# Attention, rational MLP and PReLU MLP in one kernel: shared, larger rooms for turned score halves, and mirrored and producing key chunks taken in turns

## The chip, the cores and the metric

The kernel runs on one core of one Trainium2 chip. Its time is the device time of one execution in microseconds (us). Before the change three runs gave 1598.0, 1600.2 and 1601.96 us, with a median of 1600.2 us. The rows below come from one more execution, which was profiled and took 1600.62 us.

## The reference

Three stages follow one another. Attention without softmax, in two batches of 3008 rows, model width 256, key width 64:

```python
scores = scale * np.matmul(z, z.transpose(0, 2, 1))   # scale = 1 / 3008
attn = np.maximum(scores, 0.0) ** 2
out = np.matmul(attn, v)
x = u * out
```

Then, on the 6016 rows of both batches, an MLP of hidden width 2048 with a rational activation, and a second one with a PReLU:

```python
h = x @ w_in                                          # MLP 1
P = a[0] + a[1] * h + a[2] * h2 + a[3] * h3           # h2, h3: powers of h
Q = 1.0 + np.abs(b[0]) * np.abs(h) + np.abs(b[1]) * h2
x = (P / (Q + 1e-06)) @ w_out
h = x @ w_in2                                         # MLP 2
y = (np.maximum(h, 0.0) + alpha * np.minimum(h, 0.0)) @ w_out2
```

Queries and keys are the same z, so the score matrix of a batch is symmetric: the block of queries j against keys i is the transpose of the block of queries i against keys j.

## The kernel before, in words

**Arithmetic.** Each float32 operand is split into a high and a low part (`hi`, `lo`), and a product is made of three matmuls: high by high, high by low, low by high. Splitting a tile is one cast (ACT, L118) and one subtraction (DVE, L121).

**Attention.** A batch has NQ = 6 rows (query blocks j = 0 to 5 of 512 queries, the last of 448) and NKP = 12 key chunks kp of 256 keys; chunks 2i and 2i+1 make key block i. For each chunk TensorE (PE) makes the scores (L393, L394, four matmuls into two PSUM tiles `s`), ACT applies relu (L397) and square (L400) into a tile `r` of the tag "t", ACT and DVE split it into `ahi` and `alo`, and three chunks later (LAG_A) PE adds the chunk's product with the values `vt` to the row's accumulator `acca` (12 matmuls, L437 and L446). At the end of a row DVE multiplies by u (`ut`, L482).

**Mirrored chunks, second batch alone** (`FOLD`, `folded`). A row j of the second batch makes no scores for key blocks i < j. It takes them from row i, which had made the same block the other way round: row i is then *producing*. A producing chunk (`turn_block`, L323) sends `r` through two DMA transposes as 16-bit halves into a tile `xt` (L333), and `save_turned` (L337) writes `xt` with two DMAs to a DRAM tile `rt` (L341). A mirrored chunk (`load_turned`, L346) brings the halves back into a tile `xd` with two DMAs (L351), and `a_turned` (L357) puts them together in a tile `rr` of tag "t" by a copy on ACT (L362) and one on DVE (L363). Row j has 2j mirrored chunks, 2 that lie on the diagonal, and 10 - 2j producing ones. All these DMAs are issued by SyncE (SP), in order; a wait at one of them holds all that stand behind it on SP.

**The rooms.** `xt` and `xd` have two buffers each (XT, XD). Tag "t" has six (TT), for `r` and `rr`, three tiles of each MLP step (`sq`, `ab`, `t`), and `dec`, in which a block of weights is decoded. An `r` that is producing is held until its transposes have landed; a `dec` that is spilled to DRAM (`wd`) until that DMA has landed.

**Order.** `a_stream` yields after each chunk. Beside it, `weights_due` and `spill_w` decode weights from step to step, and from step HEAD = 36 of 145 on, 40 steps of MLP 1 are spread evenly over the attention steps: PE h (L417 to L419, 12 matmuls) and PE acc (L437, L446, 12 matmuls), seven DVE operations of 128x1024. Their weights come as `w<-wd` loads from the POOL queue (L774). After the attention the rest of MLP 1 and all of MLP 2 run alone. The program is written in this order; a scheduler then orders each engine's instructions and gives each tile its buffer.

Around the change `fetch` (L675) issues the load of the next mirrored chunk, at most AHEAD = 1 beyond the one in use, and `drain` takes the rows' ends at chunks NKP-2 and NKP-1.

Of the kernel before, what the change touches and what calls it, by code (L numbers as in the profile page):

```python
# [11 lines left out]
U16 = mybir.dt.uint16  # L12
# [3 lines left out]
DRAM = bass.MemoryType.DRAM  # L16


BIG, HL, TT, RAW, ZP, XP = 24, 7, 6, 2, 8, 4

XT, XD, AHEAD = 2, 2, 1

FOLD = ((1, 0),)

# [4 lines left out]
LAG_A, LAG_M = 3, 2  # L29
# [23 lines left out]
def relu2_attention_rational_mlp_prelu_mlp(  # L53
# [15 lines left out]
    nc = tc.nc  # L69
    P = 128  # L70
# [6 lines left out]
    QB = 512  # L77
    NQ = -(-S // QB)
    NK = -(-S // P)
    NKP = NK // 2  # L80
# [15 lines left out]
    zctx = ExitStack()  # L96
    zp = zctx.enter_context(tc.tile_pool(name="zp", bufs=ZP))
    wr = zctx.enter_context(tc.tile_pool(name="wr", bufs=WR))
    xdp = zctx.enter_context(tc.tile_pool(name="xdp", bufs=XD))
    late = {}  # L100

    def raw_tile(nm, early=False):

        if early:
            return big.tile([P, 1024], F32, tag="big", name=nm)
        return tmp.tile([P, 1024], F32, tag="raw", name=nm, bufs=RAW)
# [34 lines left out]
    def load_v(b, kp):  # L141

        if b == 0:
            raw = raw_tile("vraw", True)
        else:
            raw = wr.tile([P, 1024], F32, tag="wr", name="vraw")
        r3 = raw.rearrange("p (c d) -> p c d", c=4)
        r0 = kp * 2 * P
        load_rows(r3, v[b], r0, min(S - r0, 4 * P))
        vraw[b, kp] = r3  # L150
# [97 lines left out]
    def load_z(b, g):  # L248

        raw = raw_tile("zraw", b == 0)  # L250
        n = qn[g]
        nc.sync.dma_start(out=raw[:, 0:n], in_=zt[b, :, g * QB : g * QB + n])
        if n % P:
            nc.sync.dma_start(out=raw[:, n : n + HALF], in_=zt[b, :, S - HALF : S])
            n += HALF
        t = zp.tile([P, QB], F32R, tag="z", name="zA")
        with tc.high_priority(EARLY):
            nc.vector.tensor_copy(t[:, 0:n], raw[:, 0:n])
            nc.vector.tensor_tensor(
                t[HALF:P, 0:n], raw[HALF:P, 0:n], t[HALF:P, 0:n].bitcast(F32), ALU.subtract  # L260
            )
        if (b, g) == (0, 0):
            zB[b, g] = zp.tile([P, QB], F32R, tag="z", name="zB")
            nc.scalar.copy(zB[b, g][HALF:P, 0:n], raw[HALF:P, 0:n])
            nc.vector.tensor_tensor(
                zB[b, g][0:HALF, 0:n], raw[0:HALF, 0:n], t[0:HALF, 0:n].bitcast(F32), ALU.subtract
            )
        zA[b, g] = t


    blocks = [(b, j) for b in range(B) for j in range(NQ)]
# [4 lines left out]
    xd = {}  # L276
# [39 lines left out]
    def folded(b, i, j):  # L316
        return i < j and any(b == fb and i >= f0 for fb, f0 in FOLD)

    turned = {}
    halves = {}  # L320
    unsaved = []

    def turn_block(b, j, kp, r):  # L323

        kb, k0 = kp // 2, kp % 2 * 2 * P
        if (b, j, kb) not in turned:
            turned[b, j, kb] = dr.tile([2, QB, QB], U16, name=f"rt{b}_{j}_{kb}")
        x = xdp.tile([P, 8, 2 * P], U16, tag="xt", name="xt", bufs=XT)
        ru = r.bitcast(U16)
        w = 0  # L330
        for i in range(2):
            rows = min(P, S - (2 * kp + i) * P)
            nc.sync.dma_start_transpose(out=x[:, :, w : w + rows], in_=ru[0:rows, i, :])  # L333
            w += rows
        unsaved.append((turned[b, j, kb], k0, w, x))
# [10 lines left out]
    def load_turned(b, j, kp):  # L346
        n = qn[j]
        q0 = kp % 2 * 2 * P
        d = xdp.tile([P, 2, 2, QB], U16, tag="xd", name="xd", bufs=XD)
        for h in range(2):  # L350
            nc.sync.dma_start(  # L351
                out=d[:, h, :, :n],
                in_=turned[b, kp // 2, j][h, q0 : q0 + 2 * P, :n].rearrange("(c p) k -> p c k", p=P),
            )
        halves[b, j, kp] = d
# [13 lines left out]
    def a_scores(b, j, kp):  # L369
# [43 lines left out]
        if folded(b, j, kp // 2):  # L413
            turn_block(b, j, kp, r)
# [16 lines left out]
    def pairs(acc, w, hi, lo, n, first, last, both=2):  # L431

        hi, lo = ([x[i] if type(x) is list else x[:, i, :n] for i in range(2)] for x in (hi, lo))
        for i in range(2):
            for e in range(2):
                for k in range(2):
                    nc.tensor.matmul(  # L437
                        acc[:, e, :n],
                        w[:, k, i, e * P : (e + 1) * P],
                        hi[i],  # L440
                        start=first and i == 0 and k == 0,
                        stop=False,
                    )
        for i in range(both):
            for e in range(2):
                nc.tensor.matmul(  # L446
                    acc[:, e, :n],
                    w[:, 0, i, e * P : (e + 1) * P],
                    lo[i],
                    start=False,  # L450
                    stop=last and i == both - 1,
                )

    def a_values(b, j, kp):
        n = qn[j]
        if kp == 0:

            two = j == 1 and not opened
            acc_a[b, j] = psa.tile([P, ND, QB], F32, tag=f"acc{two:d}", name="acca")
        acc = acc_a[b, j]  # L460
        hi, lo = ahl.pop((b, j, kp))
        vk = vt[b, kp]
        last = kp == NKP - 1
        pairs(acc, vk, hi, lo, n, kp == 0, last, 1 if last else 2)

    def a_u(b, j):
        n = qn[j]
        t = tmp.tile([P, ND, QB], F32, tag="raw", name="ut", bufs=RAW)
        if b == 0 and j < RAW:

            nc.gpsimd.tensor_copy(t[:, 0, 0:1], zA[0, NQ - 1][:, 0:1].bitcast(F32))
        nc.sync.dma_start(
            out=t[:, :, :n],
            in_=ut_in[b, :, j * QB : j * QB + n].rearrange("(e p) s -> p e s", p=P),
        )
        uts[b, j] = t

    def a_end(b, j):
        n = qn[j]
        t = uts.pop((b, j))  # L480
        with tc.high_priority(EARLY):
            nc.vector.tensor_tensor(t[:, :, :n], acc_a[b, j][:, :, :n], t[:, :, :n], ALU.mult)  # L482
        xd[b, j] = dr.tile([P, ND, QB], F32, name=f"xd{b}_{j}")
        nc.sync.dma_start(out=xd[b, j][:, :, :n], in_=t[:, :, :n])
# [185 lines left out]
    def a_stream():  # L670

        pend = []
        coming = [(b, j, kp) for b, j in blocks for kp in range(2 * j) if folded(b, kp // 2, j)]

        def fetch(b, j, kp):  # L675
            while coming and len(halves) < AHEAD + folded(b, kp // 2, j) and (
                coming[0][:2] == (b, j) or coming[0][:2] == (b, j + 1) and kp >= NKP - 2
            ):
                load_turned(*coming.pop(0))

        def drain(upto):
            while len(pend) > upto:
                q, kp = pend.pop(0)
                a_values(*q, kp)
                if kp == NKP - 2:
                    a_u(*q)
                if kp == NKP - 1:
                    a_end(*q)

        for q in blocks:  # L690
            b, j = q
            if q == (0, 0):
                load_z(0, 0)
                load_z(0, 1)
                load_v(0, 0)
                split_v(0, 0)
            a_begin(b, j)
            for kp in range(NKP):
                if q == (0, 0) and kp % 2 == 0:
                    for g in {0: (2,), 2: (3, 4), 4: (5,)}.get(kp, ()):  # L700
                        load_z(0, g)
                    if kp + 2 < NKP:
                        load_v(0, kp + 2)
                        split_v(0, kp + 2)
                fetch(b, j, kp)
                a_scores(b, j, kp)
                save_turned(int(folded(b, j, kp // 2)))
                pend.append((q, kp))
                drain(LAG_A)
                if j == NQ - 1 and b + 1 < B:  # L710
                    if kp % 2 == 1:
                        load_z(b + 1, kp // 2)

                k0 = kp - LAG_A - 1 if j == NQ - 1 else kp + NKP - LAG_A - 1
                b1 = b + (j == NQ - 1)
                if (j == NQ - 1 or j == 0) and 0 < b1 < B and k0 % 2 == 0:
                    if 0 <= k0 < NKP:
                        split_v(b1, k0)
                    if 0 <= k0 + 2 < NKP:
                        load_v(b1, k0 + 2)  # L720
                yield
        drain(0)
        yield

# [145 lines left out]
```

## Time and profile before

| | |
|---|---|
| median of three runs | 1600.2 us |
| the profiled execution | 1600.62 us, its span 1598.7 us |
| PE busy | 1539.4 us (96% of the span) |
| DVE busy | 1413.9 us (88%) |
| ACT busy | 1172.8 us (73%) |
| POOL busy | 90.5 us (6%) |
| DMA, queue of SP | 93.67 MB, 21.8% of 16 engines' span |
| DMA, queue of POOL | 62.94 MB, 13.4% |

An engine's busy time is the time in which it executes; PE's instructions are pipelined, so that a PE that is always busy does one matmul of 128x512 in about 0.22 us although each lasts 0.39. PEclk is the TensorE clock that was granted, as a share of full speed (2.4 GHz; 0.50 is 1.2 GHz). The DMA share is the busy time of the core's 16 DMA engines over the stretch, and can pass 1 where packets of two queues overlap on an engine. A wait is put down to what ended it. The six rows of the second batch end where DVE multiplies by u: at 421.2, 490.9, 575.1, 641.0, 710.0 and 781.1 us; the first of them begins at 340.1 us.

### The profile page before, as it was taken

What the parts mean: (1) busy time and instruction counts of PE and PEld (TensorE: products, weight loads), DVE (VectorE), ACT (ScalarE), POOL (GpSimd) and SP (SyncE); (2) the same over time, 40 slices, a digit from 0 to 9 for tenths busy, and PEclk for the clock granted to TensorE, in tenths of its full rate; (3) what the DMA queues carried; (4) which work ended last, traced back from release to release, by engine and by line L of the source; (5) the groups of instructions that cost most, each with busy time, mean ns of one, the idle gap of its engine ahead of it and who ended that gap; (6) DMA issues with size and microseconds to landing.
All of it is one profiled execution on the core that took longest, in us unless ns stands there. A gap on an engine that the chain in (4) does not pass through costs nothing.

```text
span 1598.7 us, 18271 instructions
## 1 busy us (share of the span) xinstructions
PE 1539.4 (96%) x6776; PEld 1271.4 (80%) x6776; DVE 1413.9 (88%) x1524; ACT 1172.8 (73%) x1405; POOL 90.5 (6%) x159
## 2 busy tenths in 40 slices
PE   9999999998989889888999999999999999999999
PEld 7887888786768667667788888888888888888888
DVE  8989989896979788999999998999989899998864
ACT  8989988897877878777676676667667676666644
POOL 1021000000001001101200000000000000000000
PEclk9999999998999899999999999999999999999999
DMA  6364132569897878676700010100001000001000
GB/s 203 101 208 148 59 106 73 163 148 228 235 210 209 175 221 157 192 197 214 259 2 27 27 40 1 40 12 28 27 27 40 1 27 28 35 1 40 14 1 23
DMA packets 155784, 157.76 MB, mean 99 GB/s; under 512 B 74016, under 2 KB 124720, under 8 KB 155696
## 3 DMA queue, kind: packets, MB, share of 16 engines
q1 hardware_dynamic: 134928, 93.67, 21.8%
q0 software_dynamic: 20768, 62.94, 13.4%
q8 instruction: 53, 0.87, 0.2%
q14 instruction: 35, 0.29, 0.1%
HBM read 92.94 MB, written 45.74 MB: 87 GB/s over the span
## 4 chain that ended last, share of the span: by engine, by line
PE 67%; DVE 11%; issue 9%; DMA 5%; ACT 5%; POOL 1%; SPq 0%; POOLq 0%; DVEq 0%; ACTq 0%
PE acc L437 18%; PE h L417 9%; PE h L419 9%; PE h L418 9%; PE acc L446 9%; PE acca L437 6%; PE acca L446 3%; DVE alo L121 2%; DMA wd<-dec 1%; PE s L393 1%; PE s L394 1%; DMA xt<-r 1%; PE acce L427 1%; DVE t L577 1%; ACT ahi L118 1%
## 5 line engine op out<-in xcount | busy, mean ns | idle before, releaser
L437 PE MATMUL acc<-ghi,w 128*128 128x512 f32 (+1 forms) x1472 | 365.9, 387 | 1.7 <-DVE ghi L575 1.7
L437 PEld LDWEIGHTS acc<-ghi,w 128*128 128x128 f32 x1472 | 275.3, 188 | 57.3 <-DVE ghi L575 1.6
L437 PE MATMUL acca<-ahi,vt 128*128 128x512 f32 (+1 forms) x1152 | 294.8, 394 | 10.5 <-ACT ahi L118 6.9
L417 PE MATMUL h<-xhi,w 128*128 128x512 f32 (+1 forms) x768 | 295.8, 386 | 4.1 <-DVE t L568 2.1
L418 PE MATMUL h<-xlo,w 128*128 128x512 f32 (+1 forms) x768 | 295.7, 385 | 1.1 <-DVE xlo L121 1.1
L419 PE MATMUL h<-xhi,w 128*128 128x512 f32 (+1 forms) x768 | 295.7, 385 | 0.0
L437 PEld LDWEIGHTS acca<-ahi,vt 128*128 128x128 f32 x1152 | 220.2, 192 | 58.4 <-ACT ahi L118 10.5
L446 PE MATMUL acc<-glo,w 128*128 128x512 f32 (+1 forms) x736 | 199.9, 390 | 10.5 <-DVE glo L578 10.3
L621 ACT ACTIVATE m<-h,sal 128x512 f32<-128x512 f32 (+1 forms) x192 | 127.4, 681 | 111.3 <-PE h L419 109.9
L561 ACT ACTIVATE sq<-h 128x1024 f32<-128x1024 f32 (+1 forms) x96 | 97.1, 1011 | 149.7 <-PE h L419 141.0
L417 PEld LDWEIGHTS h<-xhi,w 128*128 128x128 f32 x768 | 144.1, 188 | 35.4 <-issue 4.1
L446 PEld LDWEIGHTS acc<-glo,w 128*128 128x128 f32 x736 | 137.5, 188 | 41.9 <-DVE glo L578 14.9
L418 PEld LDWEIGHTS h<-xlo,w 128*128 128x128 f32 x768 | 144.1, 188 | 29.4 <-DVE xlo L121 1.9
L419 PEld LDWEIGHTS h<-xhi,w 128*128 128x128 f32 x768 | 144.1, 188 | 27.6
L121 DVE TENSOR_TENSOR glo<-m,ghi 128x1024 fp32r<-128x1024 f32 (+1 forms) x96 | 115.2, 1200 | 55.2 <-PE acc L437 42.0
L622 DVE SCALAR_TENSOR_TENSOR m<-h,sg,m 128x512 f32<-128x512 f32 (+1 forms) x192 | 138.1, 735 | 16.8 <-ACT m L621 15.3
L446 PE MATMUL acca<-alo,vt 128*128 128x512 f32 (+1 forms) x552 | 149.9, 389 | 0.0
L121 DVE TENSOR_TENSOR alo<-r,ahi 128x1024 fp32r<-128x1024 f32 (+2 forms) x103 | 122.9, 1195 | 17.9 <-PE acc L437 8.0
L397 ACT ACTIVATE r<-s 128x512 f32<-128x512 f32 (+1 forms) x184 | 104.2, 595 | 42.5 <-DMA xt<-r 24.3
L575 DVE SCALAR_TENSOR_TENSOR ghi<-t,sc,sq 128x1024 fp32r<-128x1024 f32 (+1 forms) x96 | 120.8, 1258 | 13.1 <-ACT sq L571 7.1
L565 DVE SCALAR_TENSOR_TENSOR ab<-sq,cb,ab 128x1024 f32<-128x1024 f32 (+1 forms) x96 | 120.8, 1258 | 9.9 <-ACT ab L562 9.7
L577 DVE SCALAR_TENSOR_TENSOR t<-t,sc,ab 128x1024 f32<-128x1024 f32 (+1 forms) x96 | 120.9, 1260 | 1.8
(96 smaller groups left out, 2222.8 us busy)
## 6 DMA issues: line engine op xcount, KB each, us to landing
w<-wd POOLq DMA_DIRECT2D x64, 512.0 KB, 4.9
rt<-xt SPq DMA_DIRECT2D x50, 256.0 KB, 3.1
wd<-dec POOLq DMA_DIRECT2D x48, 256.0 KB, 4.2
xd<-rt SPq DMA_DIRECT2D x40, 256.0 KB, 3.6
wraw<-in_moe_w_in_dram POOLq DMA_DIRECT2D x16, 512.0 KB, 4.3
wraw<-in_moe_w_out_dram POOLq DMA_DIRECT2D x16, 512.0 KB, 4.5
x2d<-x SPq DMA_DIRECT2D x11, 512.0 KB, 2.9
xr<-x2d SPq DMA_DIRECT2D x11, 512.0 KB, 3.3
```

The source lines that it names most:

```text
L121: nc.vector.tensor_tensor(dst_lo, src, dst_hi.bitcast(F32), ALU.subtract)
L397: nc.scalar.activation(r[:, i, :n], s, AF.Relu, scale=1.0 / S)
L417: nc.tensor.matmul(acc, w_hi, hi, start=first, stop=False)
L418: nc.tensor.matmul(acc, w_hi, lo, start=False, stop=False)
L419: nc.tensor.matmul(acc, w_lo, hi, start=False, stop=last)
L437: nc.tensor.matmul(acc[:, e, :n], w[:, k, i, e * P : (e + 1) * P], hi[i], start=first and i == 0 and k == 0, stop=False,)
L446: nc.tensor.matmul(acc[:, e, :n], w[:, 0, i, e * P : (e + 1) * P], lo[i], start=False, stop=last and i == both - 1,)
L565: nc.vector.scalar_tensor_tensor(ab, sq, b1, ab, ALU.mult, ALU.add)
L575: nc.vector.scalar_tensor_tensor(hi, t, a0, sq, ALU.add, ALU.mult)
L577: nc.vector.scalar_tensor_tensor(t, t, a0, ab, ALU.add, ALU.subtract)
L621: nc.scalar.activation(t[:, i], h, AF.Copy, scale=sal[:, f : f + 1])
L622: nc.vector.scalar_tensor_tensor(t[:, i], h, sg[:, f : f + 1], t[:, i], ALU.mult, ALU.max)
```

## The change

Three edits. (1) `xt` and `xd` share one tag "xx" of six buffers, and tag "t" gets seven buffers rather than six. All three kinds of tile take 4 KB of each partition, so this needs 12 KB more. (2) The ring in which POOL's queue keeps its DMA descriptors shrinks from the default of 16384 bytes of each partition to 4096, which frees those 12 KB. (3) A row of the second batch takes its mirrored chunks and the others (diagonal and producing) in turns, in proportion, and not the mirrored ones first. Where the position in the row matters and not the chunk (first and last matmul of the accumulator, u, the row's end, `fetch`, the loads of the first batch's last row), the code now goes by the position. The first batch's order stays.

With the new rule the rows of the second batch are, mirrored chunks marked with an apostrophe: row 0: 0 to 11; row 1: 2 0' 3 4 5 6 7 1' 8 9 10 11; row 2: 4 0' 5 6 1' 7 8 2' 9 10 3' 11; row 3: 6 0' 7 1' 8 2' 9 3' 10 4' 11 5'; row 5: 10 0' 1' 2' 3' 4' 11 5' 6' 7' 8' 9'. Before, all ran from 0 to 11.

```diff
-BIG, HL, TT, RAW, ZP, XP = 24, 7, 6, 2, 8, 4
-XT, XD, AHEAD = 2, 2, 1
+BIG, HL, TT, RAW, ZP, XP = 24, 7, 7, 2, 8, 4
+XX, AHEAD = 6, 1
+RING = 4096
...
-    xdp = zctx.enter_context(tc.tile_pool(name="xdp", bufs=XD))
+    xdp = zctx.enter_context(tc.tile_pool(name="xdp", bufs=XX))
...
+    def in_turns(b, j):
+        first = [kp for kp in range(NKP) if folded(b, kp // 2, j)]
+        rest = [kp for kp in range(NKP) if kp not in first]
+        order, nf = [], len(first)
+        while first or rest:
+            ahead = len(first) * (NKP - nf) > len(rest) * nf
+            order.append((first if ahead else rest).pop(0))
+        return order
+
+    order = {q: in_turns(*q) for q in blocks}
...
-        x = xdp.tile([P, 8, 2 * P], U16, tag="xt", name="xt", bufs=XT)
+        x = xdp.tile([P, 8, 2 * P], U16, tag="xx", name="xt")
...
-        d = xdp.tile([P, 2, 2, QB], U16, tag="xd", name="xd", bufs=XD)
+        d = xdp.tile([P, 2, 2, QB], U16, tag="xx", name="xd")
...
-        last = kp == NKP - 1
-        pairs(acc, vk, hi, lo, n, kp == 0, last, 1 if last else 2)
+        first, last = kp == order[b, j][0], kp == order[b, j][-1]
+        pairs(acc, vk, hi, lo, n, first, last, 1 if kp == NKP - 1 else 2)
...
-        coming = [(b, j, kp) for b, j in blocks for kp in range(2 * j) if folded(b, kp // 2, j)]
-        def fetch(b, j, kp):
+        coming = [(*q, kp) for q in blocks for kp in order[q] if folded(q[0], kp // 2, q[1])]
+        def fetch(b, j, kp, pos):
             while coming and len(halves) < AHEAD + folded(b, kp // 2, j) and (
-                coming[0][:2] == (b, j) or coming[0][:2] == (b, j + 1) and kp >= NKP - 2
+                coming[0][:2] == (b, j) or coming[0][:2] == (b, j + 1) and pos >= NKP - 2
             ):
...
-            for kp in range(NKP):
+            for pos, kp in enumerate(order[q]):
...
-    nc = _bacc.Bacc("TRN2", target_bir_lowering=False, num_devices=1)
+    nc = _bacc.Bacc("TRN2", target_bir_lowering=False, num_devices=1, dynamic_dma_scratch_size=RING)
```

How the instructions stand now, at three places. First SP in row 0 of the second batch, before, around key block 3 (in a name such as `rt1_0_3` stand the batch, the row and the key block; the numbers after `xt` and `r` tell the chunks apart):

```order
L333 DMA_TRANSPOSE xt_3259<-r_3245 128x8x128 x2
L333 DMA_TRANSPOSE xt_3291<-r_3276 128x8x128 x2
L341 DMA rt1_0_2_3185<-xt_3259 64x8x256 x2
L341 DMA rt1_0_3_3290<-xt_3291 64x8x256 x2
L333 DMA_TRANSPOSE xt_3322<-r_3308 128x8x128 x2
L351 DMA xd_3583<-rt1_0_1_3069 128x2x512
L341 DMA rt1_0_3_3290<-xt_3322 64x8x256
L333 DMA_TRANSPOSE xt_3396<-r_3381 128x8x128 x2
```

And the same place of the change:

```order
L346 DMA_TRANSPOSE xt_3259<-r_3245 128x8x128 x2
L346 DMA_TRANSPOSE xt_3291<-r_3276 128x8x128 x2
L354 DMA rt1_0_2_3185<-xt_3259 64x8x256 x2
L346 DMA_TRANSPOSE xt_3322<-r_3308 128x8x128 x2
L354 DMA rt1_0_3_3290<-xt_3291 64x8x256 x2
L354 DMA rt1_0_3_3290<-xt_3322 64x8x256 x2
L346 DMA_TRANSPOSE xt_3396<-r_3381 128x8x128 x2
L346 DMA_TRANSPOSE xt_3444<-r_3430 128x8x128 x2
```

The transposes of `r_3308` stood behind the two saves of `xt_3291`, which wait for that tile's own transposes; now they stand ahead of them.

Second, SP in row 2 of the second batch, before, from the row's loads to its third producing chunk:

```order
L351 DMA xd<-rt_0_3_3290 128x2x512 x4
L333 DMA_TRANSPOSE xt<-r 128x8x128 x4
L341 DMA rt_2_3_4475<-xt 64x8x256 x4
L333 DMA_TRANSPOSE xt<-r 128x8x128 x2
L341 DMA rt_2_4_4536<-xt 64x8x256
```

And of the change, the same producing chunks:

```order
L346 DMA_TRANSPOSE xt<-r 128x8x128 x2
L364 DMA xd<-rt_1_2_3737 128x2x512 x2
L354 DMA rt_2_3_4352<-xt 64x8x256 x2
L346 DMA_TRANSPOSE xt<-r 128x8x128 x2
L354 DMA rt_2_3_4352<-xt 64x8x256 x2
L346 DMA_TRANSPOSE xt<-r 128x8x128 x2
L364 DMA xd<-rt_1_2_3737 128x2x512 x2
```

Loads of mirrored chunks (`xd`) stood ahead of the row's transposes and behind them; now they stand between the pairs.

Third, PE at the start of row 2 of the second batch, before (`vt_2613`, `vt_2616` and `vt_2721` are the values of key chunks 0, 1 and 2, `vt_2790` and `vt_2793` those of 4 and 5):

```order
L437 MATMUL acca_4337<-ahi_4219,vt_2613 128x512 x8
L437 MATMUL acc1_3773<-ghi_4177,w_3885 128x512 x2
L446 MATMUL acca_4337<-alo_4220,vt_2613 128x512 x4
L437 MATMUL acca_4337<-ahi_4247,vt_2616 128x512 x8
L446 MATMUL acca_4337<-alo_4248,vt_2616 128x512 x4
L437 MATMUL acc1_3773<-ghi_4177,w_3885 128x512
L437 MATMUL acca_4337<-ahi_4271,vt_2721 128x512 x8
```

And of the change:

```order
L450 MATMUL acca_4356<-ahi_4223,vt_2790 128x512 x8
L459 MATMUL acca_4356<-alo_4224,vt_2790 128x512 x4
L450 MATMUL acca_4356<-ahi_4251,vt_2613 128x512 x8
L459 MATMUL acca_4356<-alo_4252,vt_2613 128x512 x4
L406 MATMUL s_4411<-zA_2649,zA_2761 128x512
L407 MATMUL s_4411<-zB_4210,zA_2761 128x512
L406 MATMUL s_4415<-zA_2649,zA_2761 128x512
L407 MATMUL s_4415<-zB_4210,zA_2761 128x512
L450 MATMUL acca_4356<-ahi_4279,vt_2793 128x512 x8
```

The row began with the products of mirrored chunks one after another; now products of a diagonal and a mirrored chunk, and new scores, follow one another.

## Rows read from the trace of the kernel before

**Rows 1.** Windows: second batch's rows 0 to 5, the rest; PEclk, DMA share, GB/s last

```profile
340.10:421.20 81.10, 73.46 (x311) 59.62 (x311) 64.24 (x65) 64.39 (x79) 6.51 (x11) 0.94 1.00 223
421.20:490.90 69.70, 63.42 (x269) 50.96 (x269) 58.61 (x62) 56.32 (x69) 4.71 (x8) 0.95 0.90 209
490.90:575.10 84.20, 74.60 (x309) 59.17 (x307) 70.26 (x78) 61.78 (x72) 9.46 (x15) 0.94 0.83 205
575.10:641.00 65.90, 61.33 (x262) 48.48 (x262) 60.57 (x65) 53.77 (x62) 5.92 (x11) 1.00 0.75 175
641.00:710.00 69.00, 60.39 (x248) 46.68 (x248) 64.07 (x76) 52.42 (x61) 6.59 (x11) 0.98 0.64 183
710.00:781.10 71.10, 64.00 (x283) 54.44 (x282) 63.56 (x65) 52.82 (x58) 10.48 (x19) 0.95 0.68 215
781.10:1598.00 816.90, 810.57 (x3654) 679.36 (x3652) 722.42 (x721) 528.39 (x622) 4.77 (x9) 1.00 0.09 29
```

**Rows 2.** Timeline of PE: start, length, the instruction, idle before it and what ended it

```profile
389.45 0.80 PE L393 MATMUL s<-zA 128*128 128x512 f32 x1 [7.38 <-ACT r L397]
...
747.37 0.80 PE L446 MATMUL acc<-glo,w 128*128 128x512 f32 x1 [4.84 <-DVE glo L578]
```

**Rows 3.** Windows around those four stalls, columns as in Rows 1

```profile
380.00:396.00 16.00, 8.62 (x29) 6.59 (x27) 10.69 (x12) 6.42 (x11) 0.00 (x0) 0.68 0.92 216
465.00:478.00 13.00, 7.44 (x25) 5.64 (x24) 7.85 (x7) 6.85 (x9) 0.00 (x0) 0.74 1.16 250
540.00:555.00 15.00, 8.36 (x25) 6.35 (x24) 7.28 (x9) 7.46 (x10) 0.07 (x1) 0.66 0.90 161
740.00:755.00 15.00, 10.16 (x37) 8.63 (x36) 11.34 (x12) 10.48 (x11) 1.07 (x2) 0.77 0.71 227
```

**Rows 4.** Waits from 340.1 to 781.1: total us, times, longest

```profile
ACT r L397 <- DMA xt<-r: 24.3, 5, 8.7
```

**Rows 5.** Timeline of ACT and of SP around 380 us

```profile
379.04 1.08 ACT L400 ACTIVATE r<-r 128x1024 f32<-128x1024 f32 x1
388.80 1.09 ACT L397 ACTIVATE r<-s 128x512 f32<-128x512 f32 x2 [8.69 <-DMA xt<-r]
...
375.70 7.41 SPq L341 DMA_DIRECT2D rt<-xt  x4
383.82 2.67 SPq L333 DMA_TRANSPOSE xt<-r  x2
```

**Rows 6.** SP's own waits, 340 to 790: total us, times, longest

```profile
SPq L351 <- DVE rr L363: 75.2, 22, 7.7
SPq L341 <- DMA xt<-r: 44.8, 23, 7.5
```

**Rows 7.** Timeline of SP, 450 to 475 and 525 to 553

```profile
460.40 10.86 SPq L333 DMA_TRANSPOSE xt<-r  x4
...
537.82 2.76 SPq L333 DMA_TRANSPOSE xt<-r  x2
548.15 0.59 SPq L341 DMA_DIRECT2D rt<-xt  x1
```

**Rows 8.** Line L333: the transposes, from issue to landing

```profile
DMA to landing us min/median/max: 3.1/4.5/9.4
```

**Rows 9.** DVE's timeline at the fourth stall, and tile xd from 736 to 750

```profile
745.54 0.67 DVE L363 COPY rr<-xd 128x896 uint16<-128x896 uint16 x1 [3.38 <-DMA xd<-rt]
...
DMA to landing us min/median/max: 2.7/5.6/8.0
```

**Rows 10.** Page: the commonest issue of POOL's queue, times, size, median us to landing

```profile
w<-wd POOLq DMA_DIRECT2D x64, 512.0 KB, 4.9
```

**Rows 11.** Waits of POOL for a load of its own, whole span

```profile
POOL w L774 <- DMA w<-wd: 9.9, 2, 6.2
```

**Rows 12.** Window of MLP steps alone, columns as in Rows 1

```profile
800.00:850.00 50.00, 49.88 (x219) 40.70 (x219) 48.47 (x47) 33.54 (x38) 0.00 (x0) 1.00 0.00 1
```

More of the change, by code (lines that the diff above doesn't have):

```diff
@@ L455, in a_values @@
         n = qn[j]
-        if kp == 0:
+        if kp == order[b, j][0]:
             two = j == 1 and not opened
@@ L684, in drain @@
                 a_values(*q, kp)
-                if kp == NKP - 2:
+                if kp == order[q][-2]:
                     a_u(*q)
-                if kp == NKP - 1:
+                if kp == order[q][-1]:
                     a_end(*q)
@@ L704, in a_stream @@
                         split_v(0, kp + 2)
-                fetch(b, j, kp)
+                fetch(b, j, kp, pos)
                 a_scores(b, j, kp)
@@ L710, in a_stream @@
                 if j == NQ - 1 and b + 1 < B:
-                    if kp % 2 == 1:
-                        load_z(b + 1, kp // 2)
-                k0 = kp - LAG_A - 1 if j == NQ - 1 else kp + NKP - LAG_A - 1
+                    if pos % 2 == 1:
+                        load_z(b + 1, pos // 2)
+                k0 = pos - LAG_A - 1 if j == NQ - 1 else pos + NKP - LAG_A - 1
                 b1 = b + (j == NQ - 1)
```

## The prediction

> **What bounds the kernel now.** I read the windows first, one for each row of the second batch and one for the rest [rows 1]. The reader is to see that after 781.1 us PE is busy for 810.57 of 816.9 us and does 3654 matmuls, 0.2236 us for each: nothing is to be had there. The six rows before it take 441.0 us for 311 + 269 + 309 + 262 + 248 + 283 = 1682 matmuls, which at 0.2236 us would need 376.1. So 64.9 us are lost there, and that is what an order of the second batch can touch.
>
> Next I read where PE stood still. Its timeline has four gaps of more than 4 us in these rows. Three are of one kind: PE waits to write new scores, because ACT has not emptied the score tiles; the first of them is 7.38 us long. The fourth, 4.84 us, waits for DVE [rows 2]. The windows around them [rows 3] give each its price, gap and aftermath together, since the granted clock there is 0.66 to 0.77 on average: each time PE comes back at 0.50 (1.2 GHz) for a while after its idle time. In 380 to 396 us 16 / 0.2236 = 71.6 matmuls would fit and 29 are there: 42.6 x 0.2236 = 9.5 us lost. In the same way 465 to 478 lost 7.4 (25 of 58.1), 540 to 555 lost 9.4 (25 of 67.1), and 740 to 755 lost 6.7 (37 of 67.1). Together 33.0 us, half of the 64.9.
>
> Then I read what these gaps wait for. ACT waited 24.3 us in five waits for transposes to land [rows 4]: the relu wants a tile of tag "t" whose last holder, a producing `r`, is not yet transposed. SP's own waits show why transposes are late [rows 6]: SP stood 44.8 us in front of saves whose transposes were under way (and nothing behind them could be issued), and 75.2 us in front of loads of mirrored chunks, until DVE had emptied one of the two `xd` buffers. The latter is harmless unless the load then lands late.
>
> **The change part by part.**
>
> *First stall, 9.5 us.* The `r` concerned is squared from 379.04 for 1.08 us, so it is ready at 380.1. Its transposes are issued at 383.82 only, behind a save that waited for the transposes of the chunk before; ACT resumes at 388.80 [rows 5]. In the new order these transposes stand ahead of that save, and six buffers leave them no save to wait for. They can go at about 380.2, some 3.6 us earlier. Besides, the seventh tile of tag "t" lets the next relu take the place of an older holder. The gap of 7.4 us shrinks by 3.6 from the first and by more from the second; nothing left would be a gain of 9.5, the first alone with its share of the slow clock 9.5 x 3.6 / 7.4 = 4.6. I take 7.5, nearer to the upper end, since the new tile works against the same wait.
>
> *Second stall, 7.4 us.* Row 1's producing chunks 4 to 7 still follow one another. Here SP needed 10.86 us to issue four transposes [rows 7], in a window with a DMA share of 1.16, so part of it is the DMA engines. Lower end: only the seventh tile helps. Six tiles serve one r and 40 / 109 of an MLP step with three tiles for each chunk, 2.1 tiles; a chunk takes 69.7 / 12 = 5.8 us, so one tile more is worth 2.8 us of patience. Upper end 7.4. I take 5.
>
> *Third stall, 9.4 us.* In row 2 the six producing chunks stood at the end, and one pair of transposes issued at 537.82 held SP until 548.15 [rows 7]. Taken in turns, they come at most two in a row, with a mirrored chunk between that adds no transpose, and the next `r` wants its tile some 5 us later, with one tile more: 5 + 2.8 = 7.8 us of the 10.3 that the pair took. Upper end 9.4, lower end 9.4 x 7.8 / 10.3 = 7.1. I take 8.
>
> *Fourth stall, 6.7 us.* DVE waited 3.38 us for a load that took up to 8.0 us to land [rows 9], and what stood behind that copy on DVE (`glo`) held PE. SP had issued the load as late as DVE freed one of two buffers [rows 6]. With six buffers, and nothing but loads left to issue by SP in most of row 5, a load can go several chunks ahead, more than the 8.0 us. Lower end 0, if other users of the six hold it back; upper end 6.7. I take 6.
>
> *The order itself.* It adds and removes no instruction: the same scores, copies and DMAs. In rows 3 to 5 mirrored chunks (no scores for PE, one more copy for DVE) and the others now share the load within a row. DVE is busy for 60.57 of 65.9, 64.07 of 69.0 and 63.56 of 71.1 us there [rows 1], against 48.47 of 50 in a window without attention [rows 12]; at that rate these rows could end at 62.5, 66.1 and 65.6, so at most 11.8 us are to be had, fourth stall included. Of the 31.9 us outside the four windows I count on nothing; the bounds are a third of it gained, 10.6, or new waits, which are a rival below. A new row begins with a chunk that needs scores, so with `zB` from a DMA; in SP's order of the change it stands a row ahead, so this is hidden, and bare it would cost one landing of some 4.5 us [rows 8] for each of five rows, 22 us.
>
> *The smaller ring.* POOL's queue moves 64 loads of 512 KB that land in 4.9 us each [rows 10], a few at a time. If a full ring made POOL wait, the nearest row is what it has waited so far for its own loads, 9.9 us [rows 11], mostly off PE's path; a gain has no way to come. I take 0. The Trainium skill (Debugging Trainium Hangs, Descriptor Overflow) warns of more descriptors on the Pool queue than the carveout holds, 16 KiB per partition, and its page DMA: Bandwidth & Descriptors (Terms) gives 16 B to a descriptor. By an estimate from these pages a quarter of the ring keeps 256 of them; no run here shows one that fills it.
>
> *Sum.* 7.5 + 5 + 8 + 6 = 26.5 us. The profiled execution took 1600.6 us (span 1598.7 and 1.9 around it), which is within 0.4 us of the median of the three runs, so the same number serves: 1600.6 - 26.5 = 1574.1, or 1574.
>
> **The rivals.**
>
> *The DMA engines are the bound, not the rooms.* Row 0 has a DMA share of 1.00 over its 81.1 us, row 1 of 0.90 [rows 1], and both keep ten and eight producing chunks almost in the old order. Then the transposes land as late as before, only from a fuller queue, and stalls one and two stay: gain 8 + 6 = 14, time 1587. Against it: in the first stall 3.6 us went by with nothing but a semaphore in the way [rows 5], and a transpose lands in 4.5 us at the median [rows 8]. The Trainium skill (DMA: Bandwidth & Descriptors, Issuing engines are not separate DMA queues) says that DMAs of all queues run on the same 16 engines and interleave, which speaks for this rival; the windows with a share over 1 agree. By it row 0 and row 1 would keep their time.
>
> *Slower: mirrored loads stuck among transposes.* Before, a mirrored chunk's load had SP and the engines nearly to itself; now 20 mirrored chunks of rows 1 to 4 have loads that queue behind transposes, which take up to 9.4 us [rows 8], and behind saves that hold SP. A late load stops DVE for 3.4 us, as it did once [rows 9], and DVE has little room in these rows. From 26.5 / 3.4 = 8 late loads on, the gain is eaten. With 11 of the 20 late the time is 1600.6 - 26.5 + 37.4 = 1612. Against it: with six buffers a load has no buffer to wait for, and `fetch` issues it before the mirrored chunk ahead of it is used, two chunks or some 11 us.
>
> *Nothing is gained.* The stalls go and the work returns elsewhere: rows 3 to 5 are near DVE's limit, and what rows 0 to 2 win is waited for there, by the scheduler's new order. Then 1598. For it speaks only that DVE is at 92% in row 3; against it, that DVE too was idle in the windows of the stalls (10.69 of 16 us busy, 7.28 of 15) [rows 3] and that rows 0 to 2 end without waiting for the others.
>
> **How the numbers follow.** Forecast 0.63, DMA bound 0.17, nothing gained 0.08, slower 0.12. The likeliest case has its own range: the lower ends of the four terms, 4.6 + 2.8 + 7.1 + 0 = 14.5, give 1586; all 33.0 and the 10.6 beside give 1557. The range from 1557 to 1598 takes in both of the middle rivals and leaves out the slower one and a little at the other end. A measurement of this kernel can tell 0.3%, 4.8 us, from no change. Faster by more than that (under 1595.4): 0.63 + 0.17 and less a little, 0.78. Within it 0.10, slower 0.12.
>
> **What the profile of the changed kernel would show.** If the steps are right, the wait of ACT's relu for transposes falls from 24.3 us to under 8; SP's wait before loads for DVE goes nearly to nothing; PE has no gap of over 4 us between 340 and the end of the attention, and PEclk stays near 1.00 there; the second batch takes about 415 us in place of 441; the stretch of MLP steps alone is as long as before. The DMA rival would show gaps of PE in rows 0 and 1 with the DMA share over 1. The slower one would show waits of the copies on ACT and DVE for `xd`, many times 3 us. I am wrong if the second batch takes over 436 us, or if the time went out of another stretch.

## The result and the profile after

The changed kernel takes 1562.33 us (median of three runs, 1561.8 to 1563.86); the ratio to the kernel before is 0.9766, with a 95% interval of 0.9744 to 0.9789. That is 37.9 us less, where 26.5 were forecast: inside the range, but the sum was too small by 11.4 us.

The profiled execution has a span of 1560.6 us. The same windows as in [rows 1], by the changed kernel's own rows of the second batch:

```profile
336.10:410.80 74.70, 72.92 (x311) 58.87 (x310) 64.72 (x65) 66.68 (x82) 6.51 (x11) 0.98 1.02 224
410.80:474.10 63.30, 63.12 (x277) 51.16 (x276) 59.80 (x64) 56.39 (x70) 4.68 (x8) 1.00 1.06 250
474.10:549.00 74.90, 71.10 (x304) 57.52 (x303) 68.11 (x76) 60.62 (x72) 8.65 (x15) 0.98 0.92 230
549.00:610.10 61.10, 60.81 (x266) 49.22 (x265) 60.14 (x65) 51.74 (x59) 5.99 (x10) 1.00 0.80 209
610.10:679.10 69.00, 61.34 (x253) 47.29 (x252) 63.41 (x75) 51.59 (x60) 6.17 (x11) 0.98 0.66 190
679.10:742.90 63.80, 59.37 (x268) 49.88 (x269) 62.79 (x65) 51.31 (x55) 12.42 (x22) 1.00 0.73 227
742.90:1560.00 817.10, 811.32 (x3657) 680.05 (x3655) 722.58 (x721) 529.53 (x624) 3.30 (x7) 1.00 0.08 28
```

Read against [rows 1], the rows 0 to 5 are shorter by 6.4, 6.4, 9.3, 4.8, 0.0 and 7.3 us, 34.2 together: 441.0 became 406.8. The stretch after them is as long as it was. The remaining 4.0 us came before them: the second batch begins at 336.1 and not at 340.1. In row 1 PE is now busy for 63.12 of 63.30 us. The granted clock of the six rows is 0.98 to 1.00, where it was 0.94 to 1.00. The DMA share of rows 0 and 1 went up, to 1.02 and 1.06.

What PE's timeline shows in place of [rows 2], its longest gaps in those rows and the one that now stands where the first stall was:

```profile
391.90 0.50 PE L406 MATMUL s<-zA 128*128 128x512 f32 x1 [1.22 <-ACT r L410]
509.44 0.50 PE L430 MATMUL h<-xhi,w 128*128 128x512 f32 x1 [3.26 <-ACT xhi L120]
658.77 0.50 PE L450 MATMUL acca<-ahi,vt 128*128 128x512 f32 x1 [3.09 <-ACT ahi L120]
```

No gap exceeds 3.3 us. The waits for DMAs that answer to [rows 4] (engine and tile, what it waited for, us, times, longest):

```profile
ACT rr L375 <- DMA xd<-rt: 13.3, 3, 5.5
DVE rr L376 <- DMA xd<-rt: 5.7, 3, 3.7
ACT r L410 <- DMA xt<-r: 5.6, 2, 3.2
```

The relu's wait for transposes fell from 24.3 to 5.6 us. In its place the copies of mirrored chunks wait 19.0 us for their loads. SP's own waits, against [rows 6]:

```profile
SPq L354 <- DMA xt<-r: 46.7, 20, 10.4
...
SPq L364 <- DVE rr L376: 12.0, 3, 11.1
```

Loads hardly wait for a buffer any more (75.2 became 12.0 us). But SP stands in front of saves, until their transposes land, as long as it did, 46.7 us against 44.8. So the length of that wait alone is not its price; what counts is what stands behind the save on SP (see the first stall, further down).

### The profile page after: what moved, and what is told of

Its sections match the earlier page's. It is cut to its first block, busy times and chain, and to the rows that moved or that the text cites. A ratio compares the mean times of both kernels' runs of the same rounds, so it can differ in the third digit from the quotient of the medians.

```text
span 1560.6 us, 18163 instructions
## 1 busy us (share of the span) xinstructions
PE 1530.8 (98%) x6776; PEld 1265.1 (81%) x6776; DVE 1411.5 (90%) x1524; ACT 1171.0 (75%) x1405; POOL 89.8 (6%) x159
## 3 DMA queue, kind: packets, MB, share of 16 engines
q0 software_dynamic: 20768, 62.94, 13.7%
## 4 chain that ended last, share of the span: by engine, by line
PE 67%; issue 12%; DVE 9%; ACT 6%; DMA 5%; POOL 1%; SPq 0%; POOLq 0%; DVEq 0%; ACTq 0%
PE acc L450 18%; PE h L430 10%; PE h L431 10%; PE h L432 10%; PE acc L459 9%; PE acca L450 5%; PE acca L459 3%; DMA xt<-r 2%; DVE alo L123 1%; PE s L406 1%; PE s L407 1%; PE acce L440 1%; ACT ahi L120 1%; DMA wraw<-in_moe_w_in_dram 1%; ACT r L410 1%
## 5 line engine op out<-in xcount | busy, mean ns | idle before, releaser
L450 PE MATMUL acca<-ahi,vt 128*128 128x512 f32 (+1 forms) x1152 | 290.0, 389 | 5.5 <-ACT ahi L120 4.4
L450 PEld LDWEIGHTS acca<-ahi,vt 128*128 128x128 f32 x1152 | 215.7, 189 | 53.0 <-ACT ahi L120 8.7
L459 PEld LDWEIGHTS acca<-alo,vt 128*128 128x128 f32 x552 | 104.1, 189 | 21.9 <-DVE alo L123 1.9
```

Of the source, the lines that this page charges most:

```text
L450: nc.tensor.matmul(acc[:, e, :n], w[:, k, i, e * P : (e + 1) * P], hi[i], start=first and i == 0 and k == 0, stop=False,)
L459: nc.tensor.matmul(acc[:, e, :n], w[:, 0, i, e * P : (e + 1) * P], lo[i], start=False, stop=last and i == both - 1,)
```

## The experiments

Eight kernels separate the change's parts. All have the small ring. The table gives the ratio to the kernel before, measured beside it, and the length of rows 0 to 5 of the second batch in the one profiled execution of each. The kernel before and the ring alone, whose times cannot be told apart, differ by up to 3.6 us in a row, so a difference of that size in a single row shows nothing by itself.

| kernel | ratio, 95% interval | median us | batch 2 begins | rows 0 to 5, us |
|---|---|---|---|---|
| before | | 1600.2 | 340.1 | 81.1, 69.7, 84.2, 65.9, 69.0, 71.1 |
| ring alone | 0.9989 [0.9975, 1.0004] | 1598.3 | 341.9 | 79.2, 69.1, 80.6, 67.5, 70.3, 72.5 |
| six for xt, xd | 0.9978 [0.9952, 1.0004] | 1598.2 | 339.6 | 84.7, 65.1, 86.8, 66.4, 67.5, 66.9 |
| seventh of t | 0.9892 [0.9872, 0.9913] | 1580.9 | 335.1 | 83.5, 63.2, 80.0, 61.8, 73.1, 67.9 |
| turns | 0.9900 [0.9876, 0.9925] | 1583.1 | 339.9 | 78.5, 64.4, 76.7, 63.0, 67.7, 68.7 |
| both rooms | 0.9852 [0.9829, 0.9875] | 1575.0 | 334.2 | 79.5, 63.8, 86.1, 62.5, 68.2, 63.3 |
| turns, six | 0.9857 [0.9838, 0.9877] | 1579.0 | 341.5 | 77.2, 64.6, 76.8, 63.0, 69.7, 66.0 |
| turns, seventh | 0.9819 [0.9769, 0.9868] | 1574.7 | 336.7 | 84.1, 67.9, 75.6, 61.6, 65.1, 69.0 |
| all (the change) | 0.9766 [0.9744, 0.9789] | 1562.3 | 336.1 | 74.7, 63.3, 74.9, 61.1, 69.0, 63.8 |

**The ring alone** (`TT` 6, `tag="xt", bufs=2`, `tag="xd", bufs=2`, chunks 0 to 11 in order; only `RING = 4096` remains).

> The kernel before with POOL's descriptor ring of 4096 bytes and nothing else changed. Theory (the ring costs nothing): 1600 us, within 0.3%, the second batch 441 us long with its four gaps. Rival (a fuller ring makes POOL wait, or the other addresses of the tiles matter): over 1605, and POOL waits for its own loads for more than the 9.9 us of before.

0.9989, its interval takes in 1, and POOL waits 8.9 us for its own loads, against 9.9. The ring costs nothing that can be measured; the rival is refuted. The four gaps of PE are there, 5.59, 5.38, 3.35 and 7.34 us long, where the kernel before had 7.38, 5.56, 6.64 and 4.84: by so much such gaps differ between two kernels whose times cannot be told apart.

**Turns alone.**

```diff
-BIG, HL, TT, RAW, ZP, XP = 24, 7, 7, 2, 8, 4
+BIG, HL, TT, RAW, ZP, XP = 24, 7, 6, 2, 8, 4
...
-        x = xdp.tile([P, 8, 2 * P], U16, tag="xx", name="xt")
+        x = xdp.tile([P, 8, 2 * P], U16, tag="xt", name="xt", bufs=2)
...
-        d = xdp.tile([P, 2, 2, QB], U16, tag="xx", name="xd")
+        d = xdp.tile([P, 2, 2, QB], U16, tag="xd", name="xd", bufs=2)
```

> Chunks in turns, with the rooms of before (two buffers each for xt and xd, six of tag t) and the small ring. Theory A (the rooms carry the gain, the order only the third stall): 1588 to 1594, ACT's relu still waits over 12 us for transposes. Theory B (the order carries it, since turns alone thin out the transposes): under 1580. Rival C (loads of mirrored chunks held up behind transposes, with no rooms to cover it): slower than 1600.

1583.1, between theories A and B, and no slowdown. The relu's wait for transposes is 7.9 us, a third of before, with the old rooms. Its profile has one gap of PE over 3 us in the second batch, the first (5.86 us); the other three are gone, with the old rooms. So the order does twice what the prediction gave it (its third stall), and C is refuted.

**The seventh buffer of tag "t" alone** (the edits of the ring alone, but `TT` 7).

> Only the seventh buffer of tag t; xt and xd with two buffers each, old order, small ring. Theory A (the wait is for a tile of tag t): 1580 to 1588, the first three gaps shrink to under 3 us each, the fourth (a late load of a mirrored chunk) stays, and the first batch ends 4 us sooner too, as in the changed kernel. Rival (the wait is for transposes held behind xt's two buffers): 1592 or more, with ACT's relu waiting over 15 us.

1580.9, as theory A has it, and the first batch ends 5.0 us sooner. But the profile does not fit A's second part: there is a gap of PE of 11.8 us in row 0, longer than any before. The relu's wait is gone (5.0 us), and instead the copies into `rr` wait for a tile and a load:

```profile
ACT rr L375 <- DMA xd<-rt: 15.4, 4, 8.2
ACT rr L375 <- DMA xt<-r: 14.5, 4, 6.1
DVE rr L376 <- DMA xt<-r: 13.8, 3, 10.2
```

**Both rooms, old order.**

```diff
-    order = {q: in_turns(*q) for q in blocks}
+    order = {q: list(range(NKP)) for q in blocks}
```

> Both rooms (seven of tag t, six shared by xt and xd), old order, small ring. Theory A: 1568 to 1578, most of the 37.9 us; what the order adds is under 10. Theory B (the order carries it): over 1585, with the third gap still there.

1575.0, theory A's interval; turns add 12.7 us to the rooms, a little more than A allowed. Its timelines of DVE and of SP near 390 us show what the rooms leave in the old order:

```profile
396.83 0.76 DVE L376 COPY rr<-xd 128x1024 uint16<-128x1024 uint16 x1 [7.94 <-DMA xd<-rt]
```

```profile
383.17 2.71 SPq L346 DMA_TRANSPOSE xt<-r  x2
385.99 1.31 SPq L354 DMA_DIRECT2D rt<-xt  x2
387.35 2.91 SPq L364 DMA_DIRECT2D xd<-rt  x2
```

This is row 0, and the load is that of row 1's first mirrored chunk, which the old order takes first in its row. It was issued behind transposes and saves and took until 396.8; DVE, in order, stood at the copy for 7.94 us, and PE for 6.45. In these rows no wait for transposes is left, and 44.2 us of waits for loads stand in its place, against 10.4 before:

```profile
ACT rr L375 <- DMA xd<-rt: 30.1, 6, 8.8
DVE rr L376 <- DMA xd<-rt: 14.1, 3, 7.9
```

**The six buffers alone** (`TT` 6, old order).

> Only the six buffers shared by xt and xd; tag t with six, old order, small ring. If the seventh buffer of tag t did all of what the rooms did to the relu's wait: about 1592 or more here (rooms 1575, seventh alone 1581, so 6 us are left for the six buffers). If the six buffers free the transposes from the saves, as the prediction had it for the first stall: 1585 or less, with the first gap under 3 us.

1598.2; its interval takes in 1. The first stall did shrink as the prediction said, from 7.38 us (5.59 with the ring alone) to 2.42, and was given back 28 us later, where a mirrored chunk's copy wanted a tile of tag "t" (its timelines of PE and of DVE):

```profile
383.96 0.50 PE L406 MATMUL s<-zA 128*128 128x512 f32 x1 [2.42 <-ACT r L410]
...
412.09 0.77 PE L430 MATMUL h<-xhi,w 128*128 128x512 f32 x1 [8.13 <-DVE t L581]
```

```profile
410.05 0.74 DVE L376 COPY rr<-xd 128x1024 uint16<-128x1024 uint16 x1 [9.96 <-DMA xt<-r]
```

**Turns and the seventh buffer; turns and the six** (the change with one of the rooms taken back).

> Chunks in turns and the seventh buffer of tag t; xt and xd with two each. If gains add up: 16.6 + 18.8 = 35.4, 1564, and the six buffers add 2 in the changed kernel. If in turns the loads need the room (a load waits for one of two xd buffers and stands before the next transposes on SP): 1572 or more.

> Chunks in turns and six buffers shared by xt and xd; tag t with six. If tag t is the scarce room in turns too: 1575 to 1582, ACT's relu waiting for transposes for 8 us or more. If turns make the seventh buffer needless: under 1568.

1574.7: the median is in the second expectation's interval (1572 or more). The profile shows what that expectation names: SP stands 54.2 us in front of loads, until DVE has emptied an `xd`, against 12.0 in the change, and the relu waits 20.3 us for transposes, against 5.6. But the runs go from 1561.5, as fast as the change, to 1579.7, and the profile is that of the slowest; so what the six buffers add to the other two parts is not settled. And 1579.0, as expected for tag "t" being scarce in turns too (the relu waits 9.2 us). Of the single gains, 1.1% for the seventh buffer, 1.0% for turns and 0.2% for the six, the sum is 2.3%, and all three give 2.34%. Within the intervals the parts add up.

**Are the DMA engines the bound?** Each save of a turned chunk written once more, to a tile nobody reads:

```diff
...
-            for h in range(2):
+            for t, h in ((t, 0), (t, 1), (t2, 0), (t2, 1)):
...
```

> The changed kernel with every save of a turned chunk written a second time, to a DRAM tile that nobody reads: 60 more DMAs of some 256 KB, half of them in rows 0 and 1's ten and eight producing chunks and the row after. If the DMA engines bound rows 0 and 1 (the rival of the prediction): each extra save costs what it occupies, some 0.9 us, so over 15 us in row 0 alone, and 1590 or more. If they do not (waits on single transposes and tiles bound them): under 1572, the rows within 3 us of the changed kernel's.

1593.1 (0.9958 [0.9932, 0.9984]): the total is the first expectation's, but row 0 is no longer. (Of the 60 further saves, 36 belong to rows 0 and 1.) Windows of rows 0 to 2:

```profile
335.60:409.50 73.90, 70.55 (x306) 56.80 (x306) 61.27 (x61) 61.67 (x78) 6.50 (x11) 1.00 1.09 251
409.50:507.50 98.00, 80.59 (x320) 61.50 (x318) 75.00 (x79) 69.24 (x83) 8.09 (x14) 0.89 1.06 265
507.50:570.80 63.30, 61.64 (x261) 48.93 (x261) 58.21 (x63) 53.09 (x64) 5.24 (x9) 0.98 1.05 262
```

Row 0 takes 73.9 us against 74.7, but it does not carry all of its 20 further saves. The DMAs issued in its window, first here (`sp` is the tile nobody reads), then in the changed kernel:

```profile
rt<-xt SPq DMA_DIRECT2D x16, 256.0 KB, 4.4
sp<-xt SPq DMA_DIRECT2D x15, 256.0 KB, 4.6
xd<-rt SPq DMA_DIRECT2D x2, 256.0 KB, 5.5
xt<-r SPq DMA_TRANSPOSE x18, 5.4
```

```profile
rt<-xt SPq DMA_DIRECT2D x18, 256.0 KB, 4.5
xd<-rt SPq DMA_DIRECT2D x4, 256.0 KB, 7.1
rt<-xt SPq DMA_DIRECT2D x2, 192.0 KB, 5.3
xt<-r SPq DMA_TRANSPOSE x20, 4.4
```

So 31 saves stand against 20, but two transposes, two loads and the rest of the saves slipped into row 1. Rows 0 and 1 together are 33.9 us longer; PE did 38 matmuls more in them, some 8.5 us, which leaves 25 us for 36 saves, 0.7 us apiece, not far from the 0.9 of the first expectation. This run therefore does not refute the prediction's first rival: it shows that the queue of these two rows has little room left. What speaks against the rival in the changed kernel is that its rows 0 and 1 became 6.4 us shorter each, at DMA shares of 1.02 and 1.06, and that PE is busy for 63.12 of 63.30 us in row 1.

More than half of the loss is at the end of row 1, where PE waited for the other half of the next row's queries, and after it for ACT:

```profile
494.36 1.19 PE L409 MATMUL s<-zB,zA 128*128 128x512 f32 x2 [4.90 <-DMA zB<-zA]
...
506.68 0.79 PE L408 MATMUL s<-zA 128*128 128x512 f32 x1 [5.11 <-ACT r L412]
```

In turns a row begins with a chunk that needs `zB`. In the changed kernel that load is early enough; with a longer queue it is not. Another 6 us are lost between 435 and 445 us, where the relu waited 5.6 us for a `dec` whose spill had not landed. How much of the 31 us the whole queue does, and how much this one load, the wait for ACT and the granted clock of 0.50 behind it, is not separated.

**Are late loads all that the old order lacks?** `rooms_both` with `AHEAD` 3.

> Both rooms in the old order, with mirrored chunks loaded up to three beyond the one in use (AHEAD 3). With AHEAD 1 this order took 1575 and its copies waited 44 us for loads. If the old order loses to turns only because its loads come late: 1566 or less, waits for loads under 15 us. If it loses because its transposes come in one run (DMA engines and tiles of tag t): 1572 to 1580.

1574.1 (0.984 [0.9784, 0.9895]), no different from 1575.0, and in the second expectation's interval. The waits for loads fell from 44.2 to 19.2 us, but 13.7 us of waits of the copies for a tile that a transpose holds came back. This speaks for the second expectation without proving it, since not every late load is gone: `fetch` still issues the first loads of a row no sooner than at the last two chunks of the row before, and the copy in row 0 waits as it did (7.94 us with `AHEAD` 1; DVE's timeline):

```profile
400.14 0.74 DVE L376 COPY rr<-xd 128x1024 uint16<-128x1024 uint16 x1 [7.87 <-DMA xd<-rt]
```

Behind it PE has a gap of 7.84 us. That the order gains by thinning out transposes too, and not by its loads alone, is argued here and not shown.

**Better versions.** The same memory, divided otherwise: `TT` 8, `XX` 5; then with `AHEAD` 2; then, with `AHEAD` 1, the row's store on POOL:

```diff
-BIG, HL, TT, RAW, ZP, XP = 24, 7, 7, 2, 8, 4
+BIG, HL, TT, RAW, ZP, XP = 24, 7, 8, 2, 8, 4
-XX, AHEAD = 6, 1
+XX, AHEAD = 5, 2
```

> The changed kernel with eight buffers of tag t and five shared by xt and xd (the same memory). If waits for a tile of tag t still cost in the changed kernel (5.6 us of relu, 5.1 of sq in its trace): 1556 to 1560. If what is left are late loads of mirrored chunks (13.3 us on ACT, 5.7 on DVE): 1561 or more, and slower if five buffers hold the loads back.

> Eight buffers of tag t, five shared by xt and xd, in turns, with loads up to two beyond the one in use. If late loads are what is left (16 us of waits in the version with AHEAD 1, which took 1561): 1552 to 1558. If the five buffers are then filled by loads that come too early, and transposes wait for them: 1563 or more.

> Eight and five in turns, AHEAD 1, and the store of a row's result (xd from ut, 12 DMAs) issued by POOL in place of SP. If loads are late because SP stands at that store until DVE has made ut (53 us of SP's waits): 1552 to 1558. If the load of MLP weights, which POOL issues, is held up instead: 1565 or more.

1561.2 (0.975 [0.9726, 0.9773]): not to be told from the change, as the second expectation has it. 1555.6 (1554.5 to 1556.3; 0.9723 [0.968, 0.9767]): loads two ahead are worth some 4 us more by the ratios and 6 by the medians, but the two intervals overlap. It is the fastest kernel of the study by its median; the copies wait 11.2 us for loads, where with one ahead they waited 16.2. Its rows 1 to 3 leave PE almost nothing to wait for (windows, as above):

```profile
410.60:473.90 63.30, 63.12 (x277) 51.06 (x276) 59.84 (x65) 55.51 (x70) 4.68 (x8) 1.00 1.03 236
473.90:541.90 68.00, 67.98 (x297) 54.79 (x296) 66.62 (x75) 60.12 (x70) 8.64 (x15) 1.00 1.03 264
541.90:603.90 62.00, 62.00 (x273) 50.26 (x272) 61.20 (x67) 53.22 (x61) 6.28 (x11) 1.00 0.79 216
```

The store on POOL gave 1564.1 (0.9782 [0.9735, 0.9829]), between its two expectations: no gain, and the copies wait 25.3 us for loads. SP's long wait for that store does not make the loads late: with the store on SP, 35.9 of the 53.3 us are one wait that begins after the last load of a mirrored chunk.

## Why the prediction was right, and where its sum fell short

*Where the time would come from.* Right: the four stalls are gone, the MLP stretch is unchanged, and the relu's wait is under 8 us. The second batch went to 406.8 and not to some 415.

*First stall (7.5).* Row 0 is shorter by 6.4 us. That this is near the term is partly luck, for the working misread its rows and was incomplete. The transposes issued at 383.82 are not those of the `r` squared from 379.04. They are those of `r_3308`, key chunk 7, in the listing of SP under "The change"; chunk 7 was squared one before, and chunk 8's transposes went at 389.46, after the stall (timelines of ACT and SP, before):

```profile
369.70 1.07 ACT L400 ACTIVATE r<-r 128x1024 f32<-128x1024 f32 x1
...
389.46 2.75 SPq L333 DMA_TRANSPOSE xt<-r  x2
```

So `r_3308` was ready at 370.8, and its transposes stood 13.0 us behind the saves of the chunks before, not 3.6. In the changed kernel the same chunk is ready at 365.2, and they go 3.2 us later:

```profile
364.12 1.06 ACT L413 ACTIVATE r<-r 128x1024 f32<-128x1024 f32 x1
...
368.36 5.30 SPq L346 DMA_TRANSPOSE xt<-r  x2
```

With the six buffers alone they go 2.0 us after the square, and the gap is 2.42 us; with turns alone, so with the old rooms, 11.7 us after it, and the gap is 5.86. The mechanism was right, then, and larger than the sum had it. But the gap cost as much again at the next wait for a tile when the six came alone. With both rooms row 0 was 79.5 us; only with all three parts 74.7. The order inside row 0 is the same in both. What differs is row 1's beginning: in turns its first chunk needs no load, so the copy of the first mirrored chunk stands later in DVE's order. DVE waits less for its load, 3.67 us in place of 7.94, and PE has no gap over 1.22 us in row 0, where it had one of 6.45:

```profile
400.02 0.76 DVE L376 COPY rr<-xd 128x1024 uint16<-128x1024 uint16 x1 [3.67 <-DMA xd<-rt]
```

I had counted turns for nothing here.

*Second stall (5).* 6.4 us in row 1; each of the three parts alone brings it to 63.2 to 65.1, from 69.1 with the ring alone, so they do not add up in this row.

*Third stall (8).* 9.3 us in row 2, and it is the order's, as said: 74.9 to 76.8 in the four kernels of the table in turns, 80.0 to 86.8 in the five in the old order.

*Fourth stall (6).* 7.3 us in row 5, most of it the rooms': 63.3 with both rooms. Turns alone leave no gap of PE over 3 us there either, but a row of 68.7.

*The order itself (0).* Mis-sized. Row 3 gained 4.8 us, more than the 3.4 that DVE's rate was to allow: DVE is now busy for 60.14 of 61.10 us, more than the 48.47 of 50 that I had taken for its limit [rows 12]. That limit was what one stretch needed of DVE, not what DVE can do. Nor is the gain the order's alone: row 3 is 61.8 us with the seventh buffer alone and 63.0 with turns alone, against 67.5 with the ring alone.

*The first batch (not in the sum).* 4.0 us. Every kernel of the table with a seventh buffer begins the second batch at 334.2 to 336.7, every one without at 339.6 to 341.9. Tag "t" serves the first batch too, and I had looked for gaps of over 4 us in the second alone. By the prediction's own test (time out of another stretch) it is wrong in this tenth of the gain.

So the parts that the sum priced came to 6.4 + 6.4 + 9.3 + 7.3 = 29.4 us against 26.5, and 8.8 us lay in two places that it priced at nothing; that makes 38.2, and row 4 and the rest give next to nothing.

*The rivals.* "The DMA engines are the bound" foretold that rows 0 and 1 would keep their time; they did not, though their DMA share rose. The run with the saves doubled shows how little room they have left. "Mirrored loads stuck among transposes" exists: a load takes 4.9 us at the median after the change and 3.8 before, and the copies wait 19.0 us for loads, 10.4 before. It does not decide, since no gap of PE that it makes is long. It comes nearest to true with the rooms and without turns, 5.5 us and 44.2 us. The Trainium skill (DMA: Bandwidth & Descriptors, Issuing engines are not separate DMA queues) says that DMAs run on the same 16 engines and interleave, whichever engine started them. The longer landings, beside a DMA share of row 1 that rose from 0.90 to 1.06, agree with it.

## What to carry to other kernels

A wait names the tile that was scarce at that moment; give it one more buffer and look at once who holds the next one. Here each room alone moved part of the wait to another user of the same queue or tag: the six buffers gained nothing that can be measured by themselves, the seventh tile 1.1% in spite of a new gap of 11.8 us. Order is a remedy of its own: turns alone gained 1.0% without any memory. And follow a tile by its number before you price a wait: two `r` beside each other in a timeline are easily taken for one. Where one row produces what another consumes over the same in-order queue, mix the two kinds of chunk, and let a row begin with one that needs nothing from that queue.

## What was not expected of the hardware

A DMA transpose can take long from issue to landing: 2.8 us at the least, 4.6 at the median and 13.3 at the most in the changed kernel, the longest in row 2, whose DMA share is 0.92. And a short wait of PE can be dear several times over. After the one of 4.90 us in the run with the saves doubled, PE did 10 matmuls in the 10 us from 495 to 505, where 45 fit at full clock. It was busy for 5.06 us of them at a granted clock of 0.50 (1.2 GHz), for work that takes 2.2 us at full clock; the larger part of the loss, 4.94 us, is new idle time, most of it the wait of 5.11 us for ACT shown above:

```profile
495.00:505.00 10.00, 5.06 (x10) 2.17 (x8) 3.39 (x3) 9.84 (x13) 0.00 (x0) 0.50 1.11 353
```
